# Where the split weights of nine block products are made: at the start of the products, or during the pass before it and through DRAM

## The chip, the core and the metric

The kernel runs on one core of a Trainium2 chip. A core has TensorE (matrix products), VectorE, ScalarE and GpSimd (element-wise work), and SyncE, whose queue issues all the DMAs here. Each engine takes its instructions in the order in which they were written. The metric is the device time of one execution in microseconds (us), and the time of a kernel is the median of several executions.

## The reference, cut to what matters

The inputs go through causal attention, then through two feed-forward layers on 2304 tokens with a model width of 512:

```
attn = softmax(q k^T / 8 + decay bias, causal) v      # 4 batches, 8 heads, 576 tokens, width 64
h  = x @ w_in                                         # 512 -> 2048
x2 = (h * clip(h + 3, 0, 6) / 6) @ w_out              # 2048 -> 512
h2 = max(x2 @ w1, x2 @ w2, x2 @ w3)                   # 512 -> 768, three times
out = h2 @ w_out2                                     # 768 -> 512
```

The weights come as 64-bit numbers and are decoded to 32-bit ones by bit operations.

## The kernel before, in words

**Products of split numbers.** Every factor is split into a high part (rounded) and a low part (the rest), and a product is three matmuls: high by high, high by low, low by high (`three`, lines 433 to 435). Tokens lie in eight units of 288 (`U1`). A matmul has 128 x 128 weights and 288 columns.

**Stages.** Attention comes first. While it runs, and behind it, the first pass of the first layer treats 6 of its 16 hidden blocks for all units (`hidden1` and `reduce1` with z = 0). The second pass (z = 1) treats the other ten: `hidden1` makes `ps_h`, `gate` turns it into the split `gt` (nine buffers), `reduce1` makes `ps_x`, and `x2_out` adds the `part` of the first pass, read back from DRAM as `pt`, and stores the unit to DRAM (`x2_d`, event `x2_stored[u]`). Then come the block products of the second layer (`hidden2`), and last the product with `w_out2` (`reduce2`).

**Block products.** Two units at a time (index t, four of them) meet nine weight pairs (index n, `PAIRS`; a pair is two of the 18 blocks of w1, w2, w3). Each pair with each t takes seven products instead of eight, of two by three matmuls each, 42 in all. That needs sums and differences of the quarters of the weights, and of x2. Both kinds are split into high and low.

- The weights' *forms*: `raw_pair` and `raw_half` decode a pair into the tile `wr`, in a buffer of the stock W, during the second pass. `form` then makes four sums (`combined`, line 1094) and six splits (`split_form`: a rounding on ScalarE or VectorE, lines 334 and 336, and a subtraction on VectorE or GpSimd, line 349), into three tiles `wf` and half of a tile `wg`. These lie in buffers of the stock W2. W2 holds the ten input and the ten output weight blocks of the second pass, and gets a buffer back when the last unit has used a block.
- The tokens' forms: `unit_forms` reads the two units of t back (`xr`), makes four differences, and `unit_form` splits seven tiles into two halves `xf` each. The buffers of `xf` (stock XFS) are eight in place of the tile x (pool mb1, when the last `hidden1` is done, event `x_over`), six former `gt` buffers, and four in place of the decoder's buffers (pool mb3).

The seven products of `hidden2` are added up in PSUM and by `pull`, `fold` and `join` on ScalarE and VectorE (`merged_out`, `third_out`, tiles `mm`, `m`, `tmp`).

**Order.** The program is written by a planner: every helper is a thread that asks for an engine (`yield "DVE", cost`), for a buffer of a stock, or for an event. The planner keeps a clock of its own with modelled costs, and hands each engine to the waiting thread with the smallest rank. The rank of the gates on VectorE is 140, of `x2_out` 200, of `hidden2` -1; threads started at NS + k have rank 160 + k, and the 6 blocks of `w_out2` (`out_weight`), which are decoded and parked in DRAM (`o2_d`), are among these. The order on the chip is then fixed; what waits there are the engines for each other, and SyncE's queue for the data and buffers of its next DMA.

**Buffers.** W has 12 buffers, RAW (a block as read) and AM (scratch of decoder and form) two each. `main` waits for `o2_stored` and `mp_over` (the last x2 store is issued), closes the decoder's pool and opens mb3, which gives two scratch tiles to AM, four buffers to XFS and one to W2.

Of the kernel before, what the change touches and what calls it, by code (L numbers as in the profile page):

```python
# [9 lines left out]
F32 = mybir.dt.float32  # L10
# [12 lines left out]
P = 128  # L23
# [8 lines left out]
HK = KD // 2 * P  # L32
NA = 6
NG = 9
WARM = 20
ORDER = 0
MOE = 160
# [166 lines left out]
def dve2(n):  # L204
    return 0.068 + n * 0.00104
# [14 lines left out]
def pool2(n):  # L220
    return 0.148 + n * 0.0021
# [36 lines left out]
def attn_moe_moe2(ctx, tc, q, k, v, s, w_in, w_out, w1, w2, w3, w_out2, out):  # L258
# [6 lines left out]
    def event():  # L265
        return Event(flow)
# [6 lines left out]
    x_d = [dram.tile([2, KD, P, S], F32R, name=f"x_d{b}") for b in range(B)]  # L273
    part_d = [dram.tile([KD, P, U1], F32, name=f"part_d{u}") for u in range(NU)]
    x2_d = [dram.tile([KD, P, U1], F32, name=f"x2_d{u}") for u in range(NU)]
    o2_d = [dram.tile([P, 2, DM], F32R, name=f"o2_d{j}") for j in range(NJ)]
    m_d = {(u, j): dram.tile([P, U1], F32, name=f"m_d{u}_{j}") for u in range(NU) for j in range(NJ)}

# [305 lines left out]
    def load(dst, src, nbytes):  # L584
        yield DMA
        copy(dst, src)
        return flow.landing(nbytes)
# [324 lines left out]
    gt_ready = {(z, u, f): event() for z in range(2) for u in range(NU) for f in range(NF)}  # L912
    part_stored = [event() for u in range(NU)]
    x2_stored = [event() for u in range(NU)]
    x_over, mp_over = event(), event()

    def load_xs():
        for z in range(2):
# [129 lines left out]
    for g in range(NJ // 2):  # L1048
        PAIRS += [((0, 2 * g), (1, 2 * g)), ((0, 2 * g + 1), (1, 2 * g + 1)), ((2, 2 * g), (2, 2 * g + 1))]
    NP2 = len(PAIRS)  # L1050
    raw_ready = [[event(), event()] for _ in range(NP2)]
    raw_item = [event() for _ in range(NP2)]
    form_ready = [event() for _ in range(NP2)]
    o2_stored = [event() for _ in range(NJ)]
    LEFT = {1: "11", 2: "12", 3: "S4", 4: "22", 5: "S1", 6: "S2", 7: "S3"}
    RIGHT = {1: "11", 2: "21", 3: "22", 4: "T4", 5: "T1", 6: "T2", 7: "T3"}
    MERGED = ((1, "A"), (7, "D"), (6, "C"), (3, "E"), (5, "A"), (4, "C"), (2, "F"))
    THIRD = ((1, "A"), (6, "C"), (7, "D"), (2, "A"), (5, "B"), (4, "D"), (3, "B"))
    FORM = (DVE + POOL, DVE)
    XFS, TMP, MF = (stock() for _ in range(3))  # L1060
    STAGE = {n: stock() for n in RIGHT.values()}

    def raw_pair(n):
        item = yield W.get()
        r = make(item, [P, 2, 512], F32, "wr")
        raw_item[n].set((r, item))

    def raw_half(n, half):
        r, _ = yield raw_item[n]
        i, j = PAIRS[n][half]  # L1070
        yield from bits_in((w1, w2, w3)[i][j], r[:, half])
        raw_ready[n][half].set()

    def out_weight(j):
        yield from decode(w_out2[j], W, ("o2", j))
# [3 lines left out]
        W.put(item)  # L1079
        o2_stored[j].set()  # L1080

    def spare_weights():
        for j in range(NJ):
            yield o2_stored[j]
        for _ in range(2 * NA - NP2):
            W2.put((yield W.get()))

    def split_form(hi, src, lo, n):
        yield from rounded(hi, src, n, ACT + DVE)
        yield from minus(lo, src, hi.bitcast(F32), n, DVE + POOL)  # L1090

    def combined(dst, a, b_, op, n):
        e = yield [("DVE", dve2(n)), ("POOL", pool2(n))]
        (vec if e == "DVE" else pool).tensor_tensor(out=dst, in0=a, in1=b_, op=op)

    forms_of = {}
    form_free = [event() for _ in range(NP2)]

    def forms():
        for n in range(NP2):  # L1100
            for half in range(2):
                yield raw_ready[n][half]
            r, ri = raw_item[n].value
            items = []
            for _ in range(3):
                items.append((yield W2.get()))
            made = [make(item, [P, 2, 2, HK], F32R, "wf") for item in items]
            if n % 2 == 0:
                spare = yield W2.get()
                single = make(spare, [P, 2, 2, HK], F32R, "wg")  # L1110
            forms_of[n] = items + ([spare] if n % 2 else [])
            flow.start(flow.cur.prio, form(n, r, ri, made, single))

    def form(n, r, ri, made, single):
# [12 lines left out]
        yield from combined(y, a12, y, ALU.subtract, HK)  # L1127
        yield from split_form(single[:, n % 2, 0], a22, single[:, n % 2, 1], HK)
        W2.put(ri)
        yield from split_form(t2[:, 1, 0], y, t2[:, 1, 1], HK)  # L1130
        AM.put(am)
        form_ready[n].set({
            "S1": t1[:, 0], "S2": t1[:, 1], "S3": t2[:, 0], "S4": t2[:, 1],
            "11": t3[:, 0], "12": t3[:, 1], "22": single[:, n % 2],
        })
        yield form_free[n]
        for item in forms_of[n]:
            W2.put(item)

    xf_ready = [{n: event() for n in STAGE} for _ in range(NUNIT)]  # L1140
    xf_free = [{n: event() for n in STAGE} for _ in range(NUNIT)]
# [242 lines left out]
    def fill(stock_, items):  # L1384
        for item in items:
            stock_.put(item)

    def main():
        yield attention_done
        pa.close()  # L1390
        w2pool = ctx.enter_context(
            tc.tile_pool(name="w2pool", bufs=1, side="right", reuse_waits="tile")
        )
        psb = ctx.enter_context(
            tc.tile_pool(name="psb", bufs=1, space=PSUM, side="right", reuse_waits="tile")
        )
# [12 lines left out]
        flow.start(0, spare_weights())  # L1409
        flow.start(NS, forms())  # L1410
        yield part_stored[NU - 1]
        fill(XF, stack(mp, "part", 2))
        fill(PT, [(px2, "t0"), (px2, "t1")])
        yield x_over
        p_mx.close()
        mb1 = ctx.enter_context(
            tc.tile_pool(name="mb1", bufs=1, side="right", reuse_waits="tile")
        )
        fill(XFS, stack(mb1, "xf", 8))
        for st in (UU, GG):  # L1420
            XF.put((yield st.get()))
            PT.put((yield st.get()))

        def halved(item, *sts):
            t = make(item, [P, 2, U1], F32, "mm")
            for x, st in enumerate(sts):
                views[item[1], x] = t[:, x]
                st.put((None, (item[1], x)))

        for sts in ((MF, MF), (TMP, TMP), (MF, TMP)):  # L1430
            halved((yield GT.get()), *sts)
        for _ in range(NG - 3):
            XFS.put((yield GT.get()))
        for j in range(NJ):
            yield o2_stored[j]
        yield mp_over
        for st in (MF, TMP, MF, MF):
            st.put((yield XF.get()))
            (MF if st is MF else TMP).put((yield PT.get()))
        for _ in range(2):  # L1440
            yield RAW.get()
            yield AM.get()
        p_dec.close()
        mb3 = p_out.enter_context(tc.tile_pool(name="mb3", bufs=1, reuse_waits="tile"))
        fill(AM, [((mb3, f"ws{x}"), None) for x in range(2)])
        fill(XFS, stack(mb3, "xf", 4))
        fill(W2, [(mb3, "w")])

    def later_weights():
        for n in range(NP2):  # L1450
            if n % 2 == 0:
                yield x2_stored[n // 2]
            flow.start(NS + 2 * NB + 2 * n, raw_pair(n))
            for half in range(2):
                flow.start(NS + 2 * NB + 2 * n + half, raw_half(n, half))
            if n > 2:
                flow.start(NS + 2 * NB + 2 * NP2 + n - 3, out_weight(n - 3))

    def late_weights():
        yield heads[WO_AFTER].ready  # L1460
# [77 lines left out]
```

## Time and profile before

| what | value |
|---|---|
| median of 3 runs | 974.1 us (972.8 to 977.03) |
| the profiled execution, as a whole | 971.03 us |
| its span, first to last instruction | 969.2 us |
| TensorE busy | 926.9 us (96%) |
| VectorE, ScalarE, GpSimd busy | 691.5, 467.5, 300.2 us |
| mean granted TensorE clock | 0.967 of full speed |
| moved by DMA | 144.55 MB |

The profile is of one execution. Busy is the time in which an engine had an instruction at work; matmuls overlap, so a busy TensorE need not be at its peak, and the count of matmuls in a stretch tells more. The mean time of one instruction contains the overlap with the next. Rows leave out the numbers in names: `x_d<-xf` is a store to `x2_d`, `o_d` is `o2_d`. A granted clock of 1.00 is 2.4 GHz, half of it 1.2 GHz.

### The profile page before, as it was taken

To read this page: it belongs to the slowest core of one execution; us is meant where nothing else is said; L and a number is where in the kernel's file an instruction comes from. 1 tells how busy PE (TensorE), PEld (TensorE's weight loads), DVE (VectorE), ACT (ScalarE), POOL (GpSimd) and SP (SyncE) were. 2 spreads that over 40 slices of the span, in tenths; PEclk is the share of its full clock that TensorE was granted. 3 is DMA by queue.
4 is the path that set the end of the run, shared out by engine and by line. 5 is a ranking of instruction groups with operands and counts; after the bars stand their busy time and mean duration, and the time that the engine had idled before them with its cause. 6 is when DMAs were issued, how large, how long until landed. Compare 5 with 4: busy or idle time off the path is not lost.

```text
span 969.2 us, 18930 instructions
## 1 busy us (share of the span) xinstructions
PE 926.9 (96%) x6532; PEld 867.4 (89%) x6532; DVE 691.5 (71%) x1880; ACT 467.5 (48%) x1172; POOL 300.2 (31%) x343
## 2 busy tenths in 40 slices
PE   9988799989989999999999999999799999999998
PEld 5545589888988999999999999998699999999998
DVE  4889889877989727998657868469977576676300
ACT  3566577676776744565334444345323232333321
POOL 5568667655656422200010000027611010021000
PEclk7789799999999999999999999999899999999999
DMA  5789777786785435664546665310212121255522
GB/s 174 186 216 264 224 189 206 182 224 165 200 218 138 148 105 191 195 205 155 166 153 218 198 212 164 113 50 14 78 58 62 53 71 42 100 173 144 163 75 74
DMA packets 87481, 144.55 MB, mean 149 GB/s; under 512 B 9532, under 2 KB 58684, under 8 KB 87384
## 3 DMA queue, kind: packets, MB, share of 16 engines
q1 hardware_dynamic: 87384, 143.33, 50.5%
q8 instruction: 52, 0.85, 0.4%
q14 instruction: 45, 0.37, 0.1%
HBM read 82.79 MB, written 33.96 MB: 120 GB/s over the span
## 4 chain that ended last, share of the span: by engine, by line
PE 71%; DMA 11%; DVE 10%; issue 3%; SPq 2%; ACT 1%; POOL 1%; DVEq 0%; POOLq 0%; ACTq 0%
PE ps_j L434 7%; PE ps_j L435 7%; PE ps_j L433 7%; PE ps_x L435 5%; PE ps_h L433 5%; PE ps_x L433 5%; PE ps_h L434 5%; PE ps_h L435 5%; PE ps_s L766 5%; PE ps_x L434 5%; DMA kt<-kb 4%; PE pt L830 3%; PE px L871 3%; PE ps_o L434 3%; PE ps_o L435 3%
## 5 line engine op out<-in xcount | busy, mean ns | idle before, releaser
L433 PE MATMUL ps_h<-x,w 128*128 128x288 f32 x512 | 153.3, 299 | 0.6 <-DVE g L963 0.6
L433 PE MATMUL ps_x<-gt,w 128*128 128x288 f32 x512 | 152.3, 297 | 0.4 <-DVE g L963 0.4
L435 PE MATMUL ps_x<-gt,w 128*128 128x288 f32 x512 | 151.3, 296 | 0.1
L434 PE MATMUL ps_h<-x,w 128*128 128x288 f32 x512 | 151.2, 295 | 0.0
L435 PE MATMUL ps_h<-x,w 128*128 128x288 f32 x512 | 150.7, 294 | 0.0
L434 PE MATMUL ps_x<-gt,w 128*128 128x288 f32 x512 | 150.3, 294 | 0.0
L434 PE MATMUL ps_j<-xf,wf 128*128 128x288 f32 x432 | 129.7, 300 | 6.5 <-POOL xf L349 3.9
L343 POOL TENSOR_SCALAR e<-e,tiny 128x256 f32<-128x256 f32 (+4 forms) x152 | 105.3, 698 | 89.8 <-DVE tiny L795 41.3
L433 PE MATMUL ps_j<-xf,wf 128*128 128x288 f32 x432 | 129.0, 299 | 0.2 <-DVE xf L336 0.2
L435 PE MATMUL ps_j<-xf,wf 128*128 128x288 f32 x432 | 128.8, 298 | 0.0
L789 ACT ACTIVATE e<-e,tiny 64x576 f32<-64x576 f32 (+4 forms) x160 | 96.2, 602 | 39.4 <-DVE tiny L781 30.2
L766 PE MATMUL ps_s<-kt,qt 66*128 66x256 f32 (+11 forms) x384 | 102.1, 362 | 11.7 <-DMA kt<-kb 6.2
L959 ACT ACTIVATE u<-ps_h,half 128x288 f32<-128x288 f32 x128 | 63.8, 498 | 78.5 <-PE ps_h L435 77.9
L433 PEld LDWEIGHTS ps_h<-x,w 128*128 128x128 f32 x512 | 96.4, 188 | 1.3 <-DVE g L963 0.9
L433 PEld LDWEIGHTS ps_x<-gt,w 128*128 128x128 f32 x512 | 96.1, 188 | 1.2 <-DVE g L963 0.6
L434 PEld LDWEIGHTS ps_h<-x,w 128*128 128x128 f32 x512 | 96.5, 188 | 0.1
L435 PEld LDWEIGHTS ps_x<-gt,w 128*128 128x128 f32 x512 | 96.2, 188 | 0.4 <-DVE w L349 0.3
L435 PEld LDWEIGHTS ps_h<-x,w 128*128 128x128 f32 x512 | 96.4, 188 | 0.0
L434 PEld LDWEIGHTS ps_x<-gt,w 128*128 128x128 f32 x512 | 96.2, 188 | 0.1
L781 DVE CUSTOM_DVE_ANT_0 e<-ps_s,above 64x288 f32<-64x288 f32 (+4 forms) x160 | 75.1, 473 | 27.5 <-PE ps_s L766 26.4
L963 DVE SCALAR_TENSOR_TENSOR g<-u,ps_h 128x288 f32<-128x288 f32 x128 | 57.3, 448 | 48.2 <-ACT u L959 47.7
L434 PEld LDWEIGHTS ps_j<-xf,wf 128*128 128x128 f32 x432 | 82.6, 191 | 7.5 <-POOL xf L349 4.1
(151 smaller groups left out, 2159.5 us busy)
## 6 DMA issues: line engine op xcount, KB each, us to landing
x<-x_d SPq DMA_DIRECT2D x64, 288.0 KB
kt<-kb SPq DMA_DIRECT2D x90, 144.0 KB
raw<-in_w_out_dram SPq DMA_DIRECT2D x22, 512.0 KB
x_d<-xs SPq DMA_DIRECT2D x16, 576.0 KB
raw<-in_w_dram SPq DMA_DIRECT2D x18, 512.0 KB
qt<-qb SPq DMA_DIRECT2D x30, 288.0 KB
raw<-in_w_in_dram SPq DMA_DIRECT2D x16, 512.0 KB
mh<-m_d SPq DMA_DIRECT2D x48, 144.0 KB
```

What stands on the lines that cost most here:

```text
L343: (pool if e == "POOL" else vec).tensor_scalar(out=y, in0=y, scalar1=r, scalar2=1.0, op0=ALU.mult, op1=ALU.mult)
L433: pe.matmul(ps, lhsT=wh, rhs=xh, start=first, stop=False, skip_group_check=again)
L434: pe.matmul(ps, lhsT=wh, rhs=xl, start=False, stop=False, skip_group_check=again)
L435: pe.matmul(ps, lhsT=wl, rhs=xh, start=False, stop=last, skip_group_check=again)
L766: pe.matmul(o, lhsT=lhs[:, qs], rhs=rhs[:, lo:hi], start=(x == 0), stop=(x == len(passes) - 1),)
L781: vec.tensor_tensor_reduce(out=e[:n, lo:hi], in0=ps[:n, 0:hi - lo], in1=above[:n, shift + lo:shift + hi], scale=-0.125, scalar=m0, op0=ALU ...
L789: act.activation(e[:n, :w], e[:n, :w], AF.Exp, bias=m0, scale=-1.0, accum_out=r,)
L830: pe.transpose(pt[:, y, :], cut, ident[:n, :n])
L871: pe.matmul(px[:, z:n], lhsT=vhl[:, x, j].rearrange("p l d -> p (l d)"), rhs=src[:, hl, x, z:n], start=(x + hl == 0), stop=(last and hl == 1),
L959: act.activation(ut, ps, AF.Relu, bias=half, scale=1.0 / 6.0)
L963: vec.scalar_tensor_tensor(out=g, in0=ut, scalar=1.0, in1=ps, op0=ALU.min, op1=ALU.mult)
```

## The change

Forms are made by VectorE and ScalarE alone, during the second pass, in W buffers. Pairs 2 to 8 are stored to DRAM (`f_d`) and read back into W2 buffers as these come free; pairs 0 and 1 (`KEPT`) stay where they were made. The blocks of `w_out2` are decoded first, from `x2_stored[0]` on; the forms follow from `x2_stored[1]`, two for each unit, in the order 2 to 8, then 0 and 1. Pool mb3 is opened by a thread of its own, `close_decoder`, that does not wait for `mp_over`. The five W buffers that are left go to W2 when all forms are made. `combined`, `split_form` and the subtraction in `unit_form` lose GpSimd.

```diff
+KEPT = 2
...
+    f_d = {n: dram.tile([4, P, 2, 2, HK], F32R, name=f"f_d{n}") for n in range(KEPT, NG2)}
...
-    FORM = (DVE + POOL, DVE)
+    FORM = (DVE, DVE)
...
     def split_form(hi, src, lo, n):
         yield from rounded(hi, src, n, ACT + DVE)
-        yield from minus(lo, src, hi.bitcast(F32), n, DVE + POOL)
+        yield from minus(lo, src, hi.bitcast(F32), n, DVE)
...
     def combined(dst, a, b_, op, n):
-        e = yield [("DVE", dve2(n)), ("POOL", pool2(n))]
-        (vec if e == "DVE" else pool).tensor_tensor(out=dst, in0=a, in1=b_, op=op)
+        yield "DVE", dve2(n)
+        vec.tensor_tensor(out=dst, in0=a, in1=b_, op=op)
...
+    def form(n):
+        ri = yield W.get()
+        r = make(ri, [P, 2, 512], F32R, "wr")
+        for half in range(2):
+            i, j = PAIRS[n][half]
+            yield from bits_in((w1, w2, w3)[i][j], r[:, half])
...
+        for _ in range(3):
+            items.append((yield W.get()))
...
+        if n < KEPT:
+            form_ready[n].set(forms_by_name(n, made, single))
+            yield form_free[n]
+            for item in items + ([spare] if n == 1 else []):
+                W2.put(item)
+            return
+        for x, t in enumerate(made):
+            yield from load(f_d[n][x], t, 8 * P * 512)
+        ev = yield from load(f_d[n][3][:, 0], single, 4 * P * 512)
+        yield ev
+        spilled[n].set()
+        for item in items + [spare]:
+            W.put(item)
+
+    def load_forms():
+        under_way = [spilled[KEPT]] * 2
+        for n in range(KEPT, NP2):
+            yield spilled[n]
...
+                items.append((yield W2.get()))
...
+            for x, t in enumerate((*made, single)):
+                yield under_way.pop(0)
+                src = f_d[n][x] if x < 3 else f_d[n][3][:, 0]
+                under_way.append((yield from load(t, src, (8 if x < 3 else 4) * P * 512)))
+            form_ready[n].set(forms_by_name(n, made, single), at=under_way[-1].time)
...
-        flow.start(NS, forms())
+        flow.start(NS, load_forms())
+        flow.start(0, close_decoder())
...
-        for j in range(NJ):
-            yield o2_stored[j]
         yield mp_over
         for st in (MF, TMP, MF, MF):
             st.put((yield XF.get()))
             (MF if st is MF else TMP).put((yield PT.get()))
+    def close_decoder():
+        yield x_closed
+        for j in range(NJ):
+            yield o2_stored[j]
+        for n in range(KEPT):
+            yield form_ready[n]
+        for n in spilled:
+            yield spilled[n]
         for _ in range(2):
             yield RAW.get()
             yield AM.get()
         p_dec.close()
         mb3 = p_out.enter_context(tc.tile_pool(name="mb3", bufs=1, reuse_waits="tile"))
-        fill(AM, [((mb3, f"ws{x}"), None) for x in range(2)])
         fill(XFS, stack(mb3, "xf", 4))
         fill(W2, [(mb3, "w")])
 
     def later_weights():
-        for n in range(NP2):
-            if n % 2 == 0:
-                yield x2_stored[n // 2]
-            flow.start(NS + 2 * NB + 2 * n, raw_pair(n))
-            for half in range(2):
-                flow.start(NS + 2 * NB + 2 * n + half, raw_half(n, half))
-            if n > 2:
-                flow.start(NS + 2 * NB + 2 * NP2 + n - 3, out_weight(n - 3))
+        yield x2_stored[0]
+        for j in range(NJ):
+            flow.start(NS + 2 * NB + j, out_weight(j))
+        for x, n in enumerate([*range(KEPT, NP2), *range(KEPT)]):
+            yield x2_stored[1 + x // 2]
+            flow.start(NS + 2 * NB + NJ + x, form(n))
```

## Rows read from the trace of the kernel before

**Rows 1.** The page: span, TensorE's busy time and instructions, DMA totals.

```profile
span 969.2 us, 18930 instructions
...
PE 926.9 (96%) x6532; PEld 867.4 (89%) x6532; DVE 691.5 (71%) x1880; ACT 467.5 (48%) x1172; POOL 300.2 (31%) x343
...
DMA packets 87481, 144.55 MB, mean 149 GB/s; under 512 B 9532, under 2 KB 58684, under 8 KB 87384
```

**Rows 2.** Windows: length; busy us (instructions) by engine; PE clock, DMA share, GB/s.

```profile
420.00:452.00 32.00, 32.00 (x243) 31.87 (x241) 29.04 (x57) 19.09 (x41) 0.00 (x0) 1.00 0.58 184
...
515.00:547.00 32.00, 32.00 (x244) 32.00 (x244) 23.36 (x49) 13.31 (x28) 0.00 (x0) 1.00 0.61 192
...
665.00:690.00 25.00, 18.27 (x117) 16.78 (x116) 24.97 (x50) 11.02 (x30) 17.84 (x19) 0.88 0.29 83
690.00:705.00 15.00, 12.98 (x82) 12.75 (x82) 14.10 (x27) 5.27 (x15) 9.31 (x9) 0.85 0.06 19
705.00:720.00 15.00, 15.00 (x115) 15.00 (x114) 11.12 (x26) 4.93 (x13) 2.94 (x3) 1.00 0.06 22
720.00:895.00 175.00, 175.00 (x1317) 175.00 (x1316) 117.87 (x280) 54.25 (x138) 15.51 (x15) 1.00 0.30 94
```

**Rows 3.** Waits of TensorE, 320 to 969 us: total us, times, longest.

```profile
PE ps_j L434 <- POOL xf L349: 3.9, 1, 3.9
PE ps_j L434 <- DVE xf L349: 2.6, 3, 1.7
PE ps_j L433 <- DVE mm L1241: 2.0, 1, 2.0
```

**Rows 4.** Timeline of TensorE, 665 to 690 us: start, length, instruction, idle before it.

```profile
665.83 0.29 PE L435 MATMUL ps_h<-x,w 128*128 128x288 f32 x1
...
680.23 0.30 PE L435 MATMUL ps_x<-gt,w 128*128 128x288 f32 x1
...
685.15 0.61 PE L434 MATMUL ps_j<-xf,wf 128*128 128x288 f32 x1 [3.94 <-POOL xf L349]
...
689.03 0.44 PE L434 MATMUL ps_j<-xf,wf 128*128 128x288 f32 x1
689.27 0.44 PE L435 MATMUL ps_j<-xf,wf 128*128 128x288 f32 x1
```

**Rows 5.** Groups by line, 420 to 720 us: busy us, mean ns, idle before.

```profile
L349 POOL TENSOR_TENSOR wf<-wr,wf 128x512 fp32r<-128x512 f32 (+1 forms) x11 | 13.4, 1217 | 139.5 <-PE ps_h L435 129.1 <-ACT wf L334 9.5 <-DVE wf L336 0.9
L349 POOL TENSOR_TENSOR wf<-ws,wf 128x256 fp32r<-128x256 f32 x11 | 10.3, 936 | 8.3 <-ACT wf L334 8.3
...
L349 DVE TENSOR_TENSOR xf<-xr,xf 128x288 fp32r<-128x288 f32 x7 | 6.1, 878 | 0.0
```

**Rows 6.** Groups by line on VectorE, 452 to 640 us.

```profile
L390 DVE SCALAR_TENSOR_TENSOR dm<-dm,raw 128x512 f32<-128x512 f32 x24 | 16.5, 688 | 8.0 <-ACT dm L388 7.3
...
L401 DVE SCALAR_TENSOR_TENSOR da<-dm,da 128x512 uint32<-128x512 uint32 x7 | 4.8, 688 | 0.1
...
L396 DVE TENSOR_SCALAR da<-dm 128x512 uint32<-128x512 uint32 x7 | 2.9, 420 | 0.0
...
L349 DVE TENSOR_TENSOR wf<-ws,wf 128x256 fp32r<-128x256 f32 x1 | 0.4, 418 | 0.0
```

**Rows 7.** Windows cut at the last x2 store of a unit, columns as in rows 2.

```profile
462.00:494.00 32.00, 32.00 (x244) 32.00 (x243) 19.86 (x42) 11.62 (x24) 0.00 (x0) 1.00 0.46 145
494.00:526.00 32.00, 32.00 (x244) 32.00 (x243) 24.86 (x45) 12.61 (x26) 4.61 (x3) 1.00 0.63 204
...
589.00:622.00 33.00, 33.00 (x252) 33.00 (x251) 20.59 (x44) 12.84 (x27) 0.00 (x0) 1.00 0.49 157
```

**Rows 8.** Window in which the six blocks of w_out2 are read back, columns as before.

```profile
840.00:860.00 20.00, 20.00 (x153) 20.00 (x152) 12.79 (x33) 5.23 (x13) 1.62 (x2) 1.00 0.72 247
```

**Rows 9.** Timeline of SyncE's queue: start, length, issue, how many merged.

```profile
652.11 23.86 SPq L309 DMA_DIRECT2D pt<-part_d  x3
...
685.77 0.33 SPq L309 DMA_DIRECT2D x_d<-xf  x1
```

More of the change, by code (lines that the diff above doesn't have):

```diff
@@ L34 @@
 NG = 9
+NG2 = 3 * NJ // 2
+KEPT = 2
 WARM = 20
@@ L914, in attn_moe_moe2 @@
     x2_stored = [event() for u in range(NU)]
-    x_over, mp_over = event(), event()
+    x_over, mp_over, x_closed = event(), event(), event()
     def load_xs():
@@ L1050, in attn_moe_moe2 @@
     NP2 = len(PAIRS)
-    raw_ready = [[event(), event()] for _ in range(NP2)]
-    raw_item = [event() for _ in range(NP2)]
     form_ready = [event() for _ in range(NP2)]
@@ L1058, in attn_moe_moe2 @@
     THIRD = ((1, "A"), (6, "C"), (7, "D"), (2, "A"), (5, "B"), (4, "D"), (3, "B"))
-    FORM = (DVE + POOL, DVE)
+    FORM = (DVE, DVE)
     XFS, TMP, MF = (stock() for _ in range(3))
     STAGE = {n: stock() for n in RIGHT.values()}
[L1063 to L1072, printed above, removed]
     def out_weight(j):
@@ L1080, in out_weight @@
         o2_stored[j].set()
-    def spare_weights():
-        for j in range(NJ):
-            yield o2_stored[j]
-        for _ in range(2 * NA - NP2):
-            W2.put((yield W.get()))
     def split_form(hi, src, lo, n):
         yield from rounded(hi, src, n, ACT + DVE)
-        yield from minus(lo, src, hi.bitcast(F32), n, DVE + POOL)
+        yield from minus(lo, src, hi.bitcast(F32), n, DVE)
     def combined(dst, a, b_, op, n):
-        e = yield [("DVE", dve2(n)), ("POOL", pool2(n))]
-        (vec if e == "DVE" else pool).tensor_tensor(out=dst, in0=a, in1=b_, op=op)
@@ L1096, in attn_moe_moe2 @@
-    forms_of = {}
+        yield "DVE", dve2(n)
+        vec.tensor_tensor(out=dst, in0=a, in1=b_, op=op)
     form_free = [event() for _ in range(NP2)]
-    def forms():
-        for n in range(NP2):
-            for half in range(2):
[L1102 to L1107, printed above, removed]
-            if n % 2 == 0:
[L1109 to L1112, printed above, removed]
@@ L1114, in form, with forms_by_name @@
-    def form(n, r, ri, made, single):
-        t1, t2, t3 = made
+    spilled = {n: event() for n in range(KEPT, NP2)}
+    shared = event()
+    def forms_by_name(n, made, single):
+        t1, t2, t3 = made
+        return {
+            "S1": t1[:, 0], "S2": t1[:, 1], "S3": t2[:, 0], "S4": t2[:, 1],
+            "11": t3[:, 0], "12": t3[:, 1], "22": single,
+        }
+    def form(n):
[4 more added lines that the diff above has]
+            yield from bits_in((w1, w2, w3)[i][j], r[:, half])
+        r = r.bitcast(F32)
+        items = []
+        for _ in range(3):
+            items.append((yield W.get()))
+        made = t1, t2, t3 = [make(item, [P, 2, 2, HK], F32R, "wf") for item in items]
+        if n == 1:
+            spare, both = yield shared
+        else:
+            spare = yield W.get()
+            both = make(spare, [P, 2, 2, HK], F32R, "wg")
+            if n == 0:
+                shared.set((spare, both))
+        single = both[:, n % 2]
@@ L1127, in form, with retire_forms, spare_weights @@
         yield from combined(y, a12, y, ALU.subtract, HK)
-        yield from split_form(single[:, n % 2, 0], a22, single[:, n % 2, 1], HK)
-        W2.put(ri)
+        yield from split_form(single[:, 0], a22, single[:, 1], HK)
+        W.put(ri)
         yield from split_form(t2[:, 1, 0], y, t2[:, 1, 1], HK)
         AM.put(am)
[L1132 to L1135, printed above, removed]
+        if n < KEPT:
[15 more added lines that the diff above has]
+            yield spilled[n]
+            items = []
+            for _ in range(3):
+                items.append((yield W2.get()))
+            made = [make(item, [P, 2, 2, HK], F32R, "wf") for item in items]
+            if n % 2 == 0:
+                spare = yield W2.get()
+                both = make(spare, [P, 2, 2, HK], F32R, "wg")
+            single = both[:, n % 2]
+            for x, t in enumerate((*made, single)):
[3 more added lines that the diff above has]
+            form_ready[n].set(forms_by_name(n, made, single), at=under_way[-1].time)
+            flow.start(flow.cur.prio, retire_forms(n, items + ([spare] if n % 2 else [])))
+    def retire_forms(n, items):
         yield form_free[n]
-        for item in forms_of[n]:
+        for item in items:
             W2.put(item)
+    def spare_weights():
+        for n in range(KEPT):
+            yield form_ready[n]
+        for n in spilled:
+            yield spilled[n]
+        for _ in range(2 * NA - 7):
+            W2.put((yield W.get()))
     xf_ready = [{n: event() for n in STAGE} for _ in range(NUNIT)]
@@ L1415, in main @@
         p_mx.close()
+        x_closed.set()
         mb1 = ctx.enter_context(
@@ L1433, in main @@
             XFS.put((yield GT.get()))
-        for j in range(NJ):
-            yield o2_stored[j]
         yield mp_over
@@ L1439, in main @@
             (MF if st is MF else TMP).put((yield PT.get()))
+    def close_decoder():
+        yield x_closed
+        for j in range(NJ):
+            yield o2_stored[j]
+        for n in range(KEPT):
+            yield form_ready[n]
+        for n in spilled:
+            yield spilled[n]
         for _ in range(2):
@@ L1449, in later_weights @@
     def later_weights():
-        for n in range(NP2):
-            if n % 2 == 0:
-                yield x2_stored[n // 2]
-            flow.start(NS + 2 * NB + 2 * n, raw_pair(n))
-            for half in range(2):
-                flow.start(NS + 2 * NB + 2 * n + half, raw_half(n, half))
-            if n > 2:
-                flow.start(NS + 2 * NB + 2 * NP2 + n - 3, out_weight(n - 3))
+        yield x2_stored[0]
[4 more added lines that the diff above has]
+            flow.start(NS + 2 * NB + NJ + x, form(n))
     def late_weights():
```

## The prediction

> **What bounds the kernel now.** I read the page first: a span of 969.2 us in which TensorE is busy for 926.9 [rows 1]. The profiled execution took 971.03 us as a whole, 1.8 more than its span; the three timed runs have a median of 974.1 us, 3.1 above it. The sum below is a difference, and I take it off the median.
>
> Then the windows by stage. From 420 us on TensorE issues 244 matmuls in 32 us, 7.62 a microsecond or 0.131 us each, all through the second pass and again from 720 to 895 [rows 2]. Only 665 to 720 is different, the passage from the second pass to the block products: 117, 82 and 115 matmuls in 55 us, 314 where 55 x 7.62 = 419 would fit. So 105 matmuls are missing, 105 x 0.131 = 13.8 us, and the granted clock is 0.88 and 0.85 in the first two stretches. This is all that can be won behind 420 us, since the rest already runs at TensorE's rate.
>
> The waits of TensorE name the stall: 3.9 us for a GpSimd xf, 2.6 for VectorE xf, 2.0 for a VectorE mm [rows 3], 8.5 together. The timeline shows the remainder: behind the 3.94 us gap matmuls follow each other at 0.24 us (689.03, 689.27) [rows 4] in place of 0.131, so the clock fell to 1.2 of 2.4 GHz after the idle time. A stretch of some 15 such matmuls costs 15 x 0.11 = 1.6 us; there is one at 687 to 691 and one behind the 2 us stall at 701, 3.2 us. 8.5 + 3.2 = 11.7, and with slower matmuls between the gaps at 685 to 687 about 13. That is near the 13.8 of the count; I use 13.
>
> Why is xf late there? The forms of the weights need W2 buffers, which come back only as the last unit of the second pass lets go of them. So most of the form work of VectorE and GpSimd falls into the end of the pass and the passage, on top of xf, the last gates, x2_out and the folds: GpSimd, without work from 589 to 622 [rows 7], is busy 17.84 of 25 us at 665 to 690, and VectorE 24.97 [rows 2]. And the two slow each other: an xf subtraction of 288 columns takes 0.878 us in this stretch [rows 5], where a 256-column subtraction of a form that ran alone took 0.418 [rows 6]. GpSimd's form subtractions take 0.94 to 1.2 us [rows 5].
>
> **The change, part by part.** *Forms leave the passage.* Each form has four sums of 256 columns (L1094), five subtractions of 256 and one of 512 (L349). On VectorE alone that is 9 x 0.418 + 0.688 (for 512 columns the nearest row is a two-input bit operation) = 4.45 us, and nine forms are 40 us [rows 6]. All of it moves from the passage to the second pass, two forms for each unit from x2_stored[1] on. In the passage VectorE keeps 14 xf halves, 14 x 0.45 = 6.3 us (ScalarE rounds), with nothing of GpSimd beside it. They are started by x_over, behind the last ps_h matmul at 665.83, and the first products run in turn with the last ps_x matmuls until 680.23 [rows 4]: the supply is faster than the use.
>
> *Buffers come earlier.* mb3's four xf buffers no longer wait for mp_over, the last x2 store at 685.77 [rows 9], but for x_over, o2 and the forms. With the eight of mb1 twelve of the 14 halves of unit 0 have room at 666; the last product, whose second matmul waited 3.94 us [rows 4], need not wait for the last gt buffers. Left over: something between 0 and the 2.6 us of VectorE xf, as the gates of the last hidden blocks still go first. I take 1.5.
>
> *The second pass gets fuller.* I cut the pass into its units, each from one unit's last x2 store to the next one's [rows 7]. A decoded half is three two-input operations of 0.688 and one of 0.420, 2.48 us of VectorE, an o2 block 3.2 with its subtraction [rows 6]. The unit 462 to 494 loses four halves and gets six o2 blocks: 19.86 - 9.9 + 19.2 = 29.2 of 32 us. The next loses an o2 block and gets two forms: 24.86 - 3.2 + 8.9 = 30.6 of 32. The one from 589 gets two halves and two forms and loses one o2: 20.59 + 5.0 + 8.9 - 3.2 = 31.3 of 33 [rows 7]. This is nearly full, but those busy times count the overlap of instructions that follow each other closely, and from 420 to 452 VectorE was busy for 29.04 of 32 us while TensorE lost nothing (243 matmuls) [rows 2]. The hidden blocks run up to nine gt buffers ahead, and gates stand before forms in the order. x2_out stands behind forms (200 against 186 to 194), but the two AM buffers let only two decode or form threads run at once, and each waits for ScalarE in between. What is late next is bounded below by nothing, above by one microsecond in each of six units: 6. The nearest row being the one at 420, I take 1.
>
> *Stores and reloads.* Seven pairs go out and come back, 3.5 x 524,288 bytes each: 12.85 MB either way, so the DMA total should rise from 144.55 [rows 1] to about 170 MB. Two pairs in 32 us are 3.67 MB. Rows of 4 KB moved 247 GB/s at a share of 0.72 [rows 8], 343 at full share, so they want 10.7 us of DMA: the share in 494 to 526 goes from 0.63 to about 0.87, an o2 block less [rows 7]. x is loaded a whole unit ahead, so it keeps its cover. pt has less: two of the four loads of a unit are issued just before they are used, and a store of 1.8 MB ahead of them would cost up to 5 us of VectorE waiting. The stores come after the forms, later in the unit than the pt loads; 0, in the 0 to 6 above.
>
> The SP queue is passed in order. It gets 56 more issues, and before the passage 23.86 us lie between the first and the last of three pt loads, whose buffers the last gates hold [rows 9]. Reloads planned behind these wait with them until 676. The five spare W buffers and the first w_in buffers let about three pairs be loaded before. Four pairs, 7.3 MB at 343 GB/s, then take 21 us and are there at 697. A pair lasts 42 x 0.131 = 5.5 us, so with pair 1 beginning at 681, pair n is wanted at 681 + 5.5 (n - 1): pair 5 at 703, pair 8 at 719.5. Hidden, with 20 us to spare: 0.
>
> *Subtractions that lose GpSimd later on.* 15.5 us of GpSimd work in 720 to 895 goes to VectorE, about 8 us at its prices, where it is busy for 118 of 175 us [rows 2]: hidden, 0.
>
> **Sum.** 13 won, 1.5 left over in the passage, 1 lost in the second pass: 10.5 us. 974.1 - 10.5 = 963.6, I say 963.5.
>
> **Rivals.** *The second pass stalls.* VectorE at 31 of 33 us is above what any row shows beside a full TensorE. If each of six units loses 1 us, and each such gap costs part of a slow-clock stretch (0.5), 9 us go and 13 - 1.5 - 9 = 2.5 remain: 971.5. For it: x2_out behind forms. Against: 420 to 452. Chance 0.10.
>
> *It doesn't do what it says.* The late xf is a matter of buffers, not of the busy VectorE: then 3.9 us and the clock stretch behind it (1.6, and about 2 of slow matmuls at 685 to 687) stay, 5.5 us are won: 968.6, at the edge of what can be told. Against: the wait ended with GpSimd's subtraction [rows 3], not with a buffer, and mb3 comes earlier. Chance 0.05, counted as same.
>
> *Slower: the reloads come late.* If all 12.85 MB stand behind the held SP queue at 676 and move at the 204 GB/s of a busy stretch [rows 7], they take 63 us, to 739, where pair 8 is wanted at 719.5: 19.5 us late. 974.1 - 10.5 + 19.5 = 983. It decides from the point where pair 8 lands after 719.5 + 10.5 = 730, below 12.85 MB / 54 us = 238 GB/s. Against: 343 for such rows, and loads that begin ahead of 676. Chance 0.10.
> The Trainium skill speaks for this rival ("DMA: Bandwidth & Descriptors", Anatomy of one DMA): it fits 2.0 us + bytes/436e3 for one DMA issued by GpSimd, so by my estimate from that page a 512 KB piece takes 3.2 us and a half piece 2.6, and the whole reload 85 us one by one, 43 us two at a time. One by one would mean 761 and over 1,000 us; two at a time, 719, no loss. No row shows one such transfer by itself; 247 GB/s at a share of 0.72 with several under way [rows 8] lies above the 164 of single pieces, so the trace speaks for overlap and I leave the chance at 0.10.
>
> **Numbers.** Less than 0.5% (4.9 us) can't be told from no change. Faster 0.75, same 0.10 + 0.05 = 0.15, slower 0.10. The likeliest case alone: from all 13.8 won (960.3, less 1.3 for the scatter below the median) to 13 - 2.6 - 6 = 4.4 won, about 959 to 969.5. The range takes in the two middle rivals, 958.5 to 972.5, and leaves out the late reloads.
>
> **What would show it.** In the profile after: 244 matmuls in 32 us in every unit from 420 on; in 665 to 720 no TensorE wait for xf above 1 us, granted clock 1.00 and over 400 matmuls; GpSimd without work behind 420; VectorE at 26 to 31 us of 32 from 490 to 620; 170 MB of DMA; the block products begin near 668 as before and end 10 us earlier. Wrong, if TensorE waits for DMA wf or wg there, if ps_x or ps_h waits for VectorE g or xf in the second pass, or if pair 0 waits for its own forms, which are made last: from x2_stored[4] and [5], the unit bounds 589 and 622 of [rows 7], with 45 us of room.

## The result, and the profile after

The changed kernel takes 960.42 us (median of 4 runs, 958.68 to 964.08), the one before 973.45 beside it: a ratio of 0.9859, 95% interval 0.9828 to 0.9889, or 13.0 us less. Every ratio in this document is the one on record, formed of undisturbed runs alone, so it can differ a little from the quotient of the medians. The profiled execution took 959.36 us with a span of 957.5, where the span before was 969.2 [rows 1].

The page of the kernel after, span, engines and DMA totals:

```profile
span 957.5 us, 18996 instructions
...
PE 924.4 (97%) x6532; PEld 868.3 (91%) x6532; DVE 692.4 (72%) x1939; ACT 468.2 (49%) x1179; POOL 231.0 (24%) x277
...
DMA packets 95544, 170.24 MB, mean 178 GB/s; under 512 B 10428, under 2 KB 59580, under 8 KB 95448
```

TensorE has the same 6532 matmuls, GpSimd 66 instructions less, and 25.7 MB more pass through DMA. Where the time came from is in the windows by stage (length; busy us and instructions of TensorE, its weight loads, VectorE, ScalarE, GpSimd; granted clock, DMA share, GB/s):

```profile
420.00:452.00 32.00, 31.96 (x242) 31.72 (x241) 28.24 (x57) 18.02 (x38) 0.00 (x0) 1.00 0.57 184
...
483.00:515.00 32.00, 32.00 (x244) 32.00 (x243) 24.66 (x51) 14.76 (x30) 0.00 (x0) 1.00 0.83 285
515.00:547.00 32.00, 32.00 (x244) 32.00 (x243) 23.87 (x57) 13.95 (x32) 0.00 (x0) 1.00 0.67 231
...
610.00:642.00 32.00, 32.00 (x245) 32.00 (x244) 29.64 (x73) 16.50 (x40) 0.00 (x0) 1.00 0.82 283
642.00:665.00 23.00, 23.00 (x177) 23.00 (x176) 15.50 (x36) 9.25 (x21) 0.00 (x0) 1.00 0.68 234
665.00:690.00 25.00, 25.00 (x191) 25.00 (x190) 17.26 (x45) 8.21 (x22) 0.00 (x0) 1.00 0.75 264
690.00:705.00 15.00, 15.00 (x115) 15.00 (x114) 10.36 (x25) 4.61 (x12) 0.00 (x0) 1.00 0.95 328
705.00:720.00 15.00, 15.00 (x115) 15.00 (x114) 7.84 (x19) 2.89 (x8) 0.00 (x0) 1.00 0.23 69
720.00:885.00 165.00, 165.00 (x1242) 165.00 (x1241) 114.98 (x282) 53.44 (x136) 0.00 (x0) 1.00 0.31 95
```

In the passage from 665 to 720 TensorE now issues 191 + 115 + 115 = 421 matmuls where it issued 314 [rows 2]: 107 more in the same 55 us, at 0.131 each 14.0 us. The granted clock is 1.00, VectorE has fallen from 24.97 to 17.26 of 25 us, GpSimd to nothing. In the second pass the count stands at 244 in 32 us as before, although VectorE has the form work there and the DMA share is up to 0.83. TensorE's waits behind 320 us are down to these (total us, times, longest):

```profile
PE ps_h L436 <- DVE g L966: 0.6, 1, 0.6
PE ps_x L436 <- DVE g L966: 0.3, 1, 0.3
PE ps_s L769 <- DMA kt<-kb: 0.3, 1, 0.3
PE ps_x L438 <- DVE w L352: 0.3, 1, 0.3
```

None is in the passage; the three that cost 8.5 us [rows 3] are gone. The difference of the spans is 11.7 us against 14.0 of the count, because executions differ by some us ahead of the point where the change begins. The kernels differ in their work from the last x2 store of the first unit on (`x2_stored[0]`). SyncE issues that store at these times, in the profiled execution of the kernel before, in that of the changed one, and in another one of the changed kernel (experiment 10):

```profile
462.09 0.32 SPq L309 DMA_DIRECT2D x_d<-xf  x1
464.33 0.32 SPq L312 DMA_DIRECT2D x_d<-xf  x1
466.48 0.32 SPq L312 DMA_DIRECT2D x_d<-xf  x1
```

The spans are 969.2, 957.5 and 959.6 us, so from that store to the end it is 507.1 us before, 493.2 after and 493.1 in the repetition. The gain from there on is 13.9 us, which is what the count says; the later start of 2.2 us belongs to the execution and not to the change.

### The profile page after: what moved, and what is told of

Same layout as the page of the kernel before. It is cut to its first block, busy times and chain, and to the rows that moved or that the text cites. A ratio compares the mean times of both kernels' runs of the same rounds, so it can differ in the third digit from the quotient of the medians.

```text
span 957.5 us, 18996 instructions
## 1 busy us (share of the span) xinstructions
PE 924.4 (97%) x6532; PEld 868.3 (91%) x6532; DVE 692.4 (72%) x1939; ACT 468.2 (49%) x1179; POOL 231.0 (24%) x277
## 2 busy tenths in 40 slices
DMA packets 95544, 170.24 MB, mean 178 GB/s; under 512 B 10428, under 2 KB 59580, under 8 KB 95448
## 4 chain that ended last, share of the span: by engine, by line
PE 70%; DMA 11%; DVE 10%; issue 3%; ACT 2%; SPq 2%; POOL 2%; DVEq 0%; POOLq 0%; ACTq 0%
PE ps_j L437 7%; PE ps_j L438 7%; PE ps_j L436 7%; PE ps_x L438 5%; PE ps_x L436 5%; PE ps_s L769 5%; PE ps_x L437 5%; PE ps_h L436 5%; PE ps_h L437 5%; PE ps_h L438 5%; DMA kt<-kb 4%; PE pt L833 3%; PE ps_o L437 3%; PE ps_o L438 3%; PE ps_o L436 3%
## 5 line engine op out<-in xcount | busy, mean ns | idle before, releaser
L437 PE MATMUL ps_j<-xf,wf 128*128 128x288 f32 x432 | 127.8, 296 | 0.0
L436 PE MATMUL ps_j<-xf,wf 128*128 128x288 f32 x432 | 127.6, 295 | 0.0
L438 PE MATMUL ps_j<-xf,wf 128*128 128x288 f32 x432 | 127.5, 295 | 0.0
L833 PE MATMUL pt<-ident,e 128*128 128x128 f32 (+1 forms) x472 | 72.6, 276 | 10.3 <-POOL e L346 6.1
```

What stands on the lines that cost most here:

```text
L436: pe.matmul(ps, lhsT=wh, rhs=xh, start=first, stop=False, skip_group_check=again)
L437: pe.matmul(ps, lhsT=wh, rhs=xl, start=False, stop=False, skip_group_check=again)
L438: pe.matmul(ps, lhsT=wl, rhs=xh, start=False, stop=last, skip_group_check=again)
L833: pe.transpose(pt[:, y, :], cut, ident[:n, :n])
```

## The experiments

The theory after the result: TensorE waited in the passage because the form work of VectorE and GpSimd was done there. Rivals: TensorE waited because xf got the buffers of mb3 late; or because VectorE and GpSimd slow each other. Two more questions: how near the second pass and the reloads are to costing something. Below, "matmuls" counts TensorE's in the windows 483 to 665 (the second pass) and 665 to 720 (the passage); ratios are to the kernel before on the same chip, whose median lay between 972.5 and 974.2. The counts are added up over the windows of the profile and can be off by one or two at their ends. Every edit also lets the planner put the instructions in a new order, so an experiment changes the order along with the work it is about.

| kernel | median us | ratio, 95% interval | matmuls 483 to 665 | 665 to 720 |
|---|---|---|---|---|
| before | 973.45 | 1 | 1388 | 314 |
| after | 960.42 | 0.9859, 0.9828 to 0.9889 | 1392 | 421 |
| 1 before, without GpSimd | 969.36 | 0.9955, 0.9935 to 0.9975 | 1387 | 339 |
| 2 after, with GpSimd | 964.76 | 0.9903, 0.9882 to 0.9924 | 1344 | 416 |
| 3 after, mb3 late | 959.28 | 0.9859, 0.9832 to 0.9885 | 1388 | 413 |
| 4 before, mb3 early | 971.68 | 0.9979, 0.9958 to 1.0000 | 1391 | 332 |
| 5 after, reloads twice | 1028.25 | 1.0567, 1.0543 to 1.0590 | 1388 | 265 |
| 6 after, stores twice | 967.20 | 0.9950, 0.9913 to 0.9987 | 1388 | 354 |
| 7 after, subtractions three times | 977.78 | 1.0054, 1.0030 to 1.0079 | 1345 | 324 |
| 8 after, copies beside reloads | 969.06 | 0.9953, 0.9929 to 0.9977 | 1392 | 356 |
| 9 after, forms a unit later | 972.99 | 0.9995, 0.9963 to 1.0028 | 1389 | 304 |
| 10 after, once more | 961.01 | 0.9840, 0.9793 to 0.9888 | 1389 | 420 |

**1. The kernel before, without GpSimd in forms.**

```diff
-    FORM = (DVE + POOL, DVE)
+    FORM = (DVE, DVE)
...
-        yield from minus(lo, src, hi.bitcast(F32), n, DVE + POOL)
+        yield from minus(lo, src, hi.bitcast(F32), n, DVE)
...
-        e = yield [("DVE", dve2(n)), ("POOL", pool2(n))]
-        (vec if e == "DVE" else pool).tensor_tensor(out=dst, in0=a, in1=b_, op=op)
+        yield "DVE", dve2(n)
+        vec.tensor_tensor(out=dst, in0=a, in1=b_, op=op)
```

> The kernel before, with the form sums, form subtractions and xf subtractions taken from GpSimd and given to VectorE, and nothing else changed: forms are still made in the passage. If the load of form work in the passage is what stalls TensorE (my theory), the stall grows: GpSimd had some 40 us of work there, at VectorE's own price about half, so some 10 us more than before, 978 to 985 us. If the two engines slowing each other is what makes xf late, the stall shrinks and the time falls to about 966.

Neither: 969.4 us, 0.45% faster. So my theory in its plain form falls: the helper GpSimd was worth less than nothing in the passage. But two thirds of the gain of the change are not reached. TensorE's waits (total, times, longest):

```profile
PE ps_j L433 <- ACT mm L1237: 5.9, 1, 5.9
PE ps_j L434 <- DVE xf L349: 1.2, 2, 0.8
```

and the window with the first of them:

```profile
690.00:705.00 15.00, 10.75 (x61) 10.76 (x62) 12.95 (x35) 4.63 (x14) 0.00 (x0) 0.77 0.09 30
```

xf is nearly in time now, and its subtraction takes 0.450 us in the passage (0.878 in [rows 5]). The stall has moved to a fold of the first products, `mm` on ScalarE, and the granted clock follows (0.77). ScalarE takes its instructions in order, and ahead of that fold its roundings wait for VectorE's sums of the forms, twice for more than 2.6 us:

```profile
687.61 0.42 ACT L334 ACTIVATE wf<-ws 128x256 fp32r<-128x256 f32 x1 [2.69 <-DVE ws L1094]
...
692.66 0.42 ACT L334 ACTIVATE wf<-ws 128x256 fp32r<-128x256 f32 x1 [2.63 <-DVE ws L1094]
...
693.81 0.39 ACT L1237 ACTIVATE mm<-ps_j 128x288 f32<-128x288 f32 x1
```

So the form work in the passage stalls TensorE without GpSimd too, by another way.

**2. The changed kernel, with GpSimd allowed again** (the lines of 1 the other way round).

> The changed kernel, with GpSimd allowed again for form sums, form subtractions and xf subtractions. If moving the form work is what counts: 959 to 963 us, as the changed kernel, since the second pass and the passage have room. If the gain is that VectorE is no longer slowed by GpSimd: half or more of it is lost, 966 to 970.

Between the two: 964.8 us, 0.44% slower than the changed kernel, a third of the gain gone. The passage is full (416 matmuls), and what is lost is lost in the second pass, 1344 for 1392, 48 x 0.131 = 6 us. The groups of VectorE, 510 to 665 us (busy us, mean ns, idle before), first here, then in the changed kernel:

```profile
L352 DVE TENSOR_TENSOR gt<-g,gt 128x288 fp32r<-128x288 f32 x48 | 26.9, 561 | 7.5 <-ACT gt L337 7.3
L966 DVE SCALAR_TENSOR_TENSOR g<-u,ps_h 128x288 f32<-128x288 f32 x48 | 21.4, 446 | 8.9 <-ACT u L962 8.9
L393 DVE SCALAR_TENSOR_TENSOR dm<-dm,raw 128x512 f32<-128x512 f32 x17 | 14.6, 860 | 12.1 <-ACT dm L391 11.9
```

```profile
L966 DVE SCALAR_TENSOR_TENSOR g<-u,ps_h 128x288 f32<-128x288 f32 x49 | 22.2, 452 | 22.0 <-ACT u L962 21.5
L352 DVE TENSOR_TENSOR gt<-g,gt 128x288 fp32r<-128x288 f32 x48 | 21.8, 454 | 5.5 <-ACT gt L337 5.3
L393 DVE SCALAR_TENSOR_TENSOR dm<-dm,raw 128x512 f32<-128x512 f32 x17 | 11.7, 690 | 2.1 <-ACT dm L391 1.4
```

The same instructions are slower in the kernel with GpSimd, 561 for 454 ns and 860 for 690, the gates come late, and TensorE waits for them:

```profile
PE ps_h L436 <- DVE g L966: 3.4, 3, 1.5
PE ps_h L436 <- DVE xf L1037: 1.6, 1, 1.6
```

The timeline shows that it is GpSimd's work at the same moment that slows them. Of the `gt` subtractions that it lists singly from 500 to 660 us, the 30 with no GpSimd instruction at work take 0.44 to 0.46 us; the 19 that overlap with one take 0.72 on average and up to 0.99. The operation `g<-u,ps_h`, which reads one of its two inputs from PSUM, takes 0.44 to 0.46 us beside GpSimd as without it.

The Trainium skill ("SBUF — State Buffer", SBUF: two separate sides) says that VectorE operations with two inputs in SBUF and GpSimd operations that read SBUF lock each other out for a whole instruction. The rows agree for VectorE: the operations with two inputs in SBUF are delayed and the one with an input in PSUM is not; they do not show for how long one is held. An operation with a single input in SBUF, `wr<-dm` in L399, is delayed as well (590 ns on average for 421).

With 1, this splits the gain. By the ratios, GpSimd out of the forms is worth 0.45% in the old place and 0.44% in the new one, and moving the forms 0.97% with GpSimd and, from 1 to the changed kernel, 0.96% without. So the two parts add, but each ratio has an interval of 0.2 to 0.3% to either side, and the counts of the single profiled executions split the gain less evenly: 24 matmuls in the old place and 53 in the new one for GpSimd, 58 and 87 for moving the forms. That both parts are there is shown; that they are independent of each other is not.

**3 and 4. The buffers of mb3, late in the changed kernel, early in the one before.**

```diff
     def close_decoder():
         yield x_closed
+        yield mp_over
```

```diff
+        flow.start(0, pass_buffers())
         for j in range(NJ):
             yield o2_stored[j]
-        yield mp_over
-        for st in (MF, TMP, MF, MF):
-            st.put((yield XF.get()))
-            (MF if st is MF else TMP).put((yield PT.get()))
...
+    def pass_buffers():
+        yield mp_over
+        for st in (MF, TMP, MF, MF):
+            st.put((yield XF.get()))
+            (MF if st is MF else TMP).put((yield PT.get()))
```

> The changed kernel, with the four xf buffers of mb3 opened only behind the last x2 store, as before. If the form load counts: 960 to 962 us, the last of the seven xf tiles being ready within a microsecond of its buffer. If the buffers count: the wait before the last product of pair 0 is back, 4 us and the slow clock behind it, 965 to 968.

> The kernel before, with mb3 opened without waiting for the last x2 store, and nothing else changed. If the form load counts: 971 to 974 us, as the kernel before, at most 3 us won. If the buffers count: 965 to 968.

Experiment 3 answers the rival: 959.3 us, the whole gain, although xf gets the buffers of mb3 only behind the last x2 store. One wait of 0.5 us for xf comes back. The early buffers are not what the gain needs.

Experiment 4, 971.7 us, is a weaker test than I meant. mb3 no longer waits for the last store, but `main` still hands out the former `gt` buffers before it opens mb3, and the first 14 halves xf are served by these six and the eight of mb1. So none of them gets a buffer earlier. The trace agrees: GpSimd's last subtraction of xf ahead of the stall is at 686.01 us where it was at 684.26, 1.7 later, as the whole execution is from the store of the first unit on (463.73 for 462.09), and the wait for it is as long as before:

```profile
PE ps_j L434 <- POOL xf L349: 4.0, 1, 4.0
PE ps_j L434 <- DVE xf L349: 3.7, 3, 1.7
```

So it is shown that the gain comes without early buffers once the forms are moved. Whether early xf buffers alone would have helped the kernel before was not tried.

**5. Every reload issued twice.**

```diff
                 src = f_d[n][x] if x < 3 else f_d[n][3][:, 0]
+                yield from load(t, src, (8 if x < 3 else 4) * P * 512)
```

> The changed kernel, with every reload of a form from DRAM issued twice, 12.85 MB more to read in the passage. In the changed kernel the last reload is issued at 699 us and the DMA share falls at 705, and pair 8 of the first t is wanted at about 720: 15 us of room. At the 405 GB/s that the reloads reached, 12.85 MB are 32 us, so pair 8 should be some 17 us late: TensorE waits for it, 972 to 982 us. If the reloads have more room than that, 959 to 963.

68 us slower than the changed kernel, far more than the bandwidth costs. The second load of a tile writes where the first does, so SyncE's queue stands until the first has landed, before every one of 28. What SyncE's queue waited for most from 650 to 788 us, while it issued them, and TensorE from 650 on (total, times, longest):

```profile
SPq L312 <- DMA wf<-f_d: 78.0, 21, 5.1
SPq L312 <- DMA wg<-f_d: 22.4, 7, 3.6
```

```profile
PE ps_j L436 <- DMA wf<-f_d: 38.1, 4, 10.3
PE ps_j L436 <- ACT mm L1270: 12.0, 2, 10.0
```

It became another experiment than I meant, that of reloads one by one: 100 us in 28 waits, 3.7 us for a piece of 512 KB and 3.2 for one of 256 KB. The prediction had a rival with such single pieces, from the Trainium skill ("DMA: Bandwidth & Descriptors", Anatomy of one DMA): an estimate of 3.2 and 2.6 us by its fit, which is for a DMA issued by GpSimd, and over 1,000 us for the kernel. The waits measured here are half a microsecond longer than that, and the time is 1028. In the changed kernel itself the pieces overlap (SyncE waits for a reload seven times from 640 to 720 us, 6.6 us in all), and the rival doesn't come about. The waits for ScalarE mm may come from the stores of m behind the reloads in the same queue; that is argued, not shown.

**8. A copy beside every reload, without a wait.** To ask for bandwidth alone, the same piece is copied from DRAM to DRAM ahead of its reload:

```diff
...
                 src = f_d[n][x] if x < 3 else f_d[n][3][:, 0]
+                dst = f_d2[n][x] if x < 3 else f_d2[n][3][:, 0]
+                yield from load(dst, src, 0)
```

> The changed kernel; ahead of each reload the same piece of the form is also copied inside DRAM, from where the reload reads it to a second place that is never read: 12.85 MB more read and written in the passage, with no wait between a reload and its copy. If the reloads have room in DMA bandwidth as long as they overlap (405 GB/s reached, 15 us between the last landing and the use of pair 8), about half of the added 32 to 37 us is covered, and the kernel takes 970 to 985 us. If only waits for single reloads cost, as in the kernel that issued every reload twice into one buffer, and the copies run beside them, 959 to 964.

969.1 us, just below the 970 expected if bandwidth counts: twice the reading and 12.85 MB of writing cost 8 to 9 us. DMA is full from 665 to 720 (shares 1.01 to 1.03, 381 to 389 GB/s). TensorE's waits, the longest and the one for a reload:

```profile
PE ps_j L437 <- DVE xf L1038: 2.9, 1, 2.9
...
PE ps_j L437 <- DMA wf<-f_d: 0.3, 1, 0.3
```

The last reload is issued at 723 instead of 699, and TensorE waits 0.3 us for one of the last pieces, at 726: the room of the reloads is just used up. What costs first is something else, x2_out: VectorE waited 6.8 us for one pt that stood behind the copies.

**6 and 7. Stores twice, and VectorE's form subtractions three times.**

```diff
...
         for x, t in enumerate(made):
+            yield from load(f_d2[n][x], t, 8 * P * 512)
+        yield from load(f_d2[n][3][:, 0], single, 4 * P * 512)
+        for x, t in enumerate(made):
             yield from load(f_d[n][x], t, 8 * P * 512)
```

```diff
         yield from minus(lo, src, hi.bitcast(F32), n, DVE)
+        if src.dtype == F32 and n in (HK, 2 * HK):
+            yield from minus(lo, src, hi.bitcast(F32), n, DVE)
+            yield from minus(lo, src, hi.bitcast(F32), n, DVE)
```

> The changed kernel, with every form stored to DRAM twice (to a second place that is never read), 12.85 MB more to write in the second pass, where the DMA share is 0.44 to 0.83. If DMA is covered there: 959 to 963 us. If the pt loads behind the stores decide (the rival that the second pass stalls): x2_out comes late and TensorE waits in several units, 965 to 975.

> The changed kernel, with every subtraction of a form's split made three times, 50 us more of VectorE work in the second pass, with the same results. VectorE was busy 24 to 30 of 32 us in its units, with some 45 us free between 462 and 655. If the second pass has the room that I counted, the forms end just about in time: 960 to 966 us. If a full VectorE makes gates and x2_out late, TensorE waits in the second pass: 970 to 985.

With the stores doubled, the second pass keeps its 1388 matmuls at DMA shares up to 0.91, so pt and x2_out cost nothing there; but 7 us by the medians (9 by the ratios) are lost in the passage, in a wait for forms that are still being made. With three subtractions it is the same and more, 17 us (19 by the ratios): a wait of 7.0 for forms and five of 5.1 in all for gates in the second pass. First the waits with doubled stores, then with three subtractions:

```profile
PE ps_j L437 <- ACT wf L338: 5.9, 1, 5.9
PE ps_j L439 <- DVE wf L353: 0.8, 1, 0.8
```

```profile
PE ps_j L438 <- DVE wf L352: 7.0, 1, 7.0
PE ps_h L436 <- DVE g L966: 5.1, 5, 1.2
```

Reloaded forms carry the name wf too, but they come by DMA; forms that wait for ScalarE or VectorE are those of pairs 0 and 1, which are kept and are made last. So what gives way first is the end of the row of forms. (In 6 the doubled stores keep W buffers longer, which would delay the later forms; that link was not tried by itself.)

**9. Every form begun one unit later.**

```diff
-            yield x2_stored[1 + x // 2]
+            yield x2_stored[2 + x // 2]
```

> The changed kernel, with every form begun one unit (31 us) later. In the changed kernel the last subtraction of pair 1's forms is at 661.8 us and pair 1's products begin at 680, 18 us of room. If that is the margin of the order in which forms are made, pair 1 is some 13 us late and TensorE waits: 968 to 978 us. If the 45 us that the prediction gave it is right, nothing changes: 959 to 963.

973.0 us: the whole gain is gone, by a single wait.

```profile
PE ps_j L436 <- ACT wf L337: 12.4, 1, 12.4
```

Pair 0 is done by then; pair 1 waits. Its last form subtraction ends the row, in the changed kernel and here:

```profile
661.79 0.42 DVE L352 TENSOR_TENSOR wf<-ws,wf 128x256 fp32r<-128x256 f32 x1
687.75 0.42 DVE L352 TENSOR_TENSOR wf<-ws,wf 128x256 fp32r<-128x256 f32 x1
```

This execution is 8.3 us ahead of the other at the last x2 store of the first unit (456.01 against 464.33), so counted from that store the subtraction is 34.3 us later and not 26. That costs a wait of 12.4 us: 22 us of room. In the changed kernel's own trace pair 1's turn comes at 680.49, 19 us behind the subtraction. So the room is some 19 to 22 us, and not the 45 that the prediction gave.

**10. The changed kernel once more**, on the chip of 8 and 9.

> The changed kernel itself, beside the other two on one chip: 958 to 963 us.

961.0 us. No experiment gave a version that is faster than the changed kernel beyond its interval; behind 320 us TensorE waits for 1.5 us in all, so little is left there.

## Why the prediction was right

The forecast was 963.5 us, 10.5 less than before; 13.0 less were measured, inside the range, a little more than forecast. The interval of the ratio is 11 to 17 us, so the terms are compared with the 13.9 us that the traces show from the first unit's last x2 store on.

- **The size of the stall.** The prediction had 11.7 and "about 13" from waits (8.5) and slow clock (3.2), and 13.8 from the count, and took 13. The traces show 13.9 and the count after 14.0. So the count of matmuls in a window was the better of the two; the waits and the clock alone leave some out.
- **What was left over: 1.5 in the passage.** Measured 0: no wait for xf at all. **Lost in the second pass: 1.** Measured 0: 1392 matmuls against 1388. These two terms and the 0.8 between 13 and the count make up the 3.4 us by which the forecast fell short of the traces, to 0.1.
- **The cause, forms in the passage.** Right, by 1 and 2: moving them is worth 0.96 to 0.97%. But the prediction counted the work and named the mutual slowing only beside it; taking GpSimd out is about a third of the gain, and the rest needs the move.
- **Buffers come earlier.** That mb3 opens earlier did not matter: experiment 3 takes it back and loses nothing that can be told. The rival in which the late xf is a matter of buffers is out as an account of the gain; what early buffers would do in the kernel before stays open.
- **The second pass gets fuller.** VectorE is busy 23.8 to 29.6 of 32 us, as forecast (26 to 31) or a bit less; its fullest stretch between the last stores of two units is from 596 to 633, 34.75 of 37 us with TensorE at its full rate:

```profile
596.00:633.00 37.00, 37.00 (x282) 37.00 (x282) 34.75 (x82) 19.39 (x45) 0.00 (x0) 1.00 0.71 239
```

One reason given for its harmlessness was wrong: that x2_out would slip in between two threads of forms. It did not. The timeline of VectorE in the changed kernel, the third x2_out of a unit, the form work behind it, and the fourth x2_out:

```profile
558.64 0.46 DVE L1037 TENSOR_TENSOR xf<-ps_x,pt 128x288 f32<-128x288 f32 x1
559.03 0.46 DVE L352 TENSOR_TENSOR gt<-g,gt 128x288 fp32r<-128x288 f32 x1
559.41 0.69 DVE L404 SCALAR_TENSOR_TENSOR wr<-dm,wr 128x512 uint32<-128x512 uint32 x1
...
570.95 0.42 DVE L352 TENSOR_TENSOR wg<-wr,wg 128x256 fp32r<-128x256 f32 x1
571.29 0.45 DVE L1037 TENSOR_TENSOR xf<-ps_x,pt 128x288 f32<-128x288 f32 x1
```

The fourth comes 12.7 us after the third, behind decodes, forms and gates (140 and 186 to 194 go ahead of 200). The mechanism of the first rival is there, then, but no wait of TensorE stands in that stretch: here it costs nothing. What TensorE lives on meanwhile (gt buffers, PSUM banks) was not tried.
- **Stores and reloads.** 170.24 MB, as worked out. The queue was held by the pt loads as said: SyncE's timeline has three pairs and two more tiles issued by 666, and then nothing until the pt loads.

```profile
664.00 1.61 SPq L312 DMA_DIRECT2D wf<-f_d  x2
675.73 1.29 SPq L312 DMA_DIRECT2D pt<-part_d  x2
...
699.49 0.32 SPq L312 DMA_DIRECT2D wg<-f_d  x1
```

The last reload leaves at 699.49, and DMA calms down by 705 to 710; 697 was forecast for the landing, against the need at 720. The late-reload rival, at 983 us, needed single pieces or half the bandwidth; experiments 5 and 8 show both prices.
- **The room of pairs 0 and 1.** "45 us" was counted from the start of their forms to the passage, as if the forms took no time; it is some 19 to 22, by experiment 9. This step was wrong without effect, and that it had none is luck: had the forms begun one unit later, the gain would have been gone.
- **The start of the block products.** They were to begin near 668, as before (669.13); they begin at 674.11, 2.2 of it the later execution. TensorE fills the time with matmuls of the second pass, so this too is without effect.

## What to carry to other kernels

Count matmuls by window before and after a stage change: here the missing matmuls times their spacing (13.8 us) gave the gain in the traces (13.9), and the sum of the waits (8.5) was short. Compare spans from the point where the change begins, since executions differ ahead of it. Work that crowds a change of stage can be moved into a stage where its engine has room, even through DRAM, if no single transfer is waited for and the piece needed first is made with room to spare; look for the room at the end of that row, not at its bandwidth. A second engine that helps with two-input work on the same memory may slow the first by more than it takes over: try the work on one engine alone, as experiments 1 and 2 did.

## What the runs showed of the hardware that I had not expected

- Reloads in rows of 4 KB reached 405 to 408 GB/s, at a share of 1.02 to 1.03, in stretches of 5 us, where 343 had been worked out from a share of 0.72 [rows 8]. The windows of the changed kernel:

```profile
660.00:665.00 5.00, 5.00 (x40) 5.00 (x40) 2.00 (x6) 1.75 (x4) 0.00 (x0) 1.00 1.03 405
...
700.00:705.00 5.00, 5.00 (x40) 5.00 (x39) 2.65 (x6) 1.11 (x3) 0.00 (x0) 1.00 1.02 408
```

- GpSimd's help had a negative worth: taking it away from the forms, with all their work left to VectorE, won 4.4 us in the kernel before (experiment 1).
- VectorE's subtraction with both inputs in SBUF took 0.44 to 0.46 us with GpSimd idle and 0.72 on average beside a GpSimd instruction, where the operation that reads PSUM took 0.44 to 0.46 either way (experiment 2).
- A single reload that is waited for costs 3.7 us for 512 KB, where one of many overlapping costs 1.3 (524,288 bytes at 405 GB/s).
